# Two unused pads of 128 bytes among the SBUF tiles of a spatial mixing stage

## The chip, the core and the metric

The kernel runs on one core of one Trainium2 chip, as one launch. The metric is device time in microseconds, and what is compared is the median of several runs. Five engines work side by side and meet at semaphores: TensorE (PE in the profile; its weight loads are listed apart as PEld), VectorE (DVE), ScalarE (ACT), GpSimd (POOL) and SyncE (SP). Here SP only issues DMAs; POOL and ACT issue some as well.

SBUF is the on-chip memory from which TensorE reads both operands of a matmul. A tile takes the same range of bytes in each of 128 partitions, so one start address per tile says where it lies. This document speaks of the start modulo 256 bytes, as "the place in the slot".

## The reference, cut to what matters

A two-dimensional Fourier transform (its real part), an expert layer with the ELU nonlinearity, and a gated layer whose gate mixes the 3072 positions of a sequence with one 3072 by 3072 matrix. There are 4 sequences of 256 numbers per position. The last function holds the stage that is changed, the einsum.

```python
X = np.fft.fft(np.fft.fft(x, axis=1), axis=2).real          # x: 4 x 3072 x 256
h = X.reshape(4 * 3072, 256) @ w_in                         # 256 -> 2048
x = np.where(h > 0, h, np.exp(np.minimum(h, 0)) - 1) @ w_out  # back to 256

def _moe2_ref(x, w_in, w_spatial, b_spatial, w_out):
    h = np.maximum(x @ w_in, 0.0)                           # 256 -> 1024
    u, v = (h[..., :512], h[..., 512:])
    v_n = (v - mean(v)) / np.sqrt(var(v) + 1e-06)
    v_s = np.einsum('ts,bsd->btd', w_spatial, v_n) + b_spatial[None, :, None]
    return (u * v_s) @ w_out                                # 512 -> 256
```

## The kernel before

The kernel is written in one order per engine by hand (a manual schedule): what stands earlier in the program is issued earlier on its engine, and semaphores carry the dependencies. It has three stages.

1. *First transforms* (to about 120 us). Folded rows of x are multiplied by tables of cosines and sines (`to`, `te`) with plain float32 matmuls, at lines 399 to 418, in tiles named pa.
2. *Expert layer and the first half of the gated layer* (to about 1196 us). Twelve blocks of 1024 positions go through eight steps each. Every product here is made by `matmul3` (line 207), three float32r matmuls on operands split into a high and a low part: high by high, low by high, high by low. Its outputs are named pe and po (function s1), acc (s2), pv (v_piece) and pu (u_piece). Four steps of this stage also hold two matmuls each in tiles named own, whose weights are a tile of 8 columns, self (line 847). The first block's second product uses plain float32 matmuls at line 713. The normalised v and the gate's other factor u go to DRAM.
3. *Spatial stage* (to the end). The 3072 by 3072 matrix is cut into 3 by 3 blocks, and for each of two pairs of sequences the 18 block products of the direct way are replaced by 15 products of sums of blocks (PRODUCTS). With 2 chunks of 512 output positions and 4 steps of 256 input positions that gives 2 x 15 x 2 x 4 = 240 units. A unit has 8 calls of `matmul3`, so 24 matmuls of 128 x 128 weights and 512 columns.

For a unit, SP loads one to three tiles raw (512 KB each), DVE adds them (line 1004), ScalarE casts the sum to whi (line 1014) and DVE subtracts to get wlo (line 1020). The tiles vhi and vlo come in the same way once for two units. In the matmuls whi and wlo are the moving operand (`rhs`) and vhi and vlo the weights (`lhsT`), written to PSUM tiles named a. When a sum is complete, DVE multiplies it by u, it is split into gh and gl (lines 1081, 1085), and `project` multiplies it by the weights wo2: there gh and gl are the moving operand.

The SBUF tiles of this stage come from pools that are opened, before the expert layer has ended, at the right-hand (upper) end of SBUF, and each new pool lies below the one before: gq (gh, gl), wq (whi, wlo), cp (wo2), th (vhi, vlo), raw, and vt for the last block of the stage before. Each of their tiles is a multiple of 2048 bytes, so all tiles in one pool have the same place in the slot. The sums, u and the bias come from other pools at the left-hand end.

Of the kernel before, what the change touches and what calls it, by code (L numbers as in the profile page):

```python
# [9 lines left out]
F32 = mybir.dt.float32  # L10
# [5 lines left out]
P = 128  # L16
# [12 lines left out]
HB = BLK // 2  # L29
# [115 lines left out]
def fourier_ffn_gated_kernel(ctx: ExitStack, tc: tile.TileContext, t, out: bass.AP):  # L145
# [138 lines left out]
    with ExitStack() as ph:  # L284
        pool = lambda n, **k: ph.enter_context(tc.tile_pool(name=n, reuse_waits="tile", **k))
# [283 lines left out]
    def pool(name, stack=ffn, **k):  # L569
        return stack.enter_context(tc.tile_pool(name=name, reuse_waits="tile", **k))  # L570
# [381 lines left out]
    def pool(name, **k):  # L952
        return ctx.enter_context(tc.tile_pool(name=name, reuse_waits="tile", **k))

    gq = pool("gq", bufs=1, side="right")
    wq = pool("wq", bufs=1, side="right")
    cp = pool("cp", bufs=1, side="right")
    th = pool("th", bufs=VB, side="right")
    rp = pool("raw", bufs=1, side="right")
# [393 lines left out]
```

## Time and profile before

| | |
|---|---|
| Median of 3 runs | 2643.21 us (2640.79 to 2643.89) |
| The profiled execution | 2641.98 us |
| Its span, first to last instruction | 2640.2 us |
| TensorE busy, share of the span | 2615.8 us, 99% |
| DVE busy | 2038.1 us, 77% |
| ScalarE busy | 1262.5 us, 48% |
| GpSimd busy | 495.1 us, 19% |
| Read from and written to HBM | 399.68 MB and 172.06 MB, 217 GB/s over the span |
| The chain that ended last | 91% of it on TensorE |

The busy time of an engine is the time in which it has at least one instruction under way. Matmuls are pipelined, so the mean duration of one (389 ns for 512 columns) is longer than the distance between the starts of two that follow each other. The distance is what a stream of matmuls costs. It is read from a list of instructions in order of time, or as the length of a window divided by the matmuls that start in it.

### The profile page before, as it was taken

The page shows a single profiled execution, that of the slowest core. Times are in us where ns is not written, and L with a number is a line of the kernel's source. Part 1 is how long each engine was busy: PE and PEld are TensorE (multiplying, and loading weights), DVE is VectorE, ACT ScalarE, POOL GpSimd, SP SyncE. Part 2 cuts the span into 40 slices and gives each one's busy share as a digit, 9 for nine tenths or more (in the row PEclk, how much of TensorE's full clock was granted, in tenths as well). Part 3 has the DMA queues.
Part 4 walks back from the last instruction along what each step waited for, and adds up shares of the span by engine and source line. Part 5 has one row for each costly group of instructions (what it writes and reads, how often), then busy time and mean ns, then how long its engine had stood idle before and what let it go on. Part 6 is the DMA issues. An engine that isn't in the chain of part 4 may idle for free.

```text
span 2640.2 us, 31514 instructions
## 1 busy us (share of the span) xinstructions
PE 2615.8 (99%) x11270; PEld 2110.0 (80%) x11270; DVE 2038.1 (77%) x2311; ACT 1262.5 (48%) x1558; POOL 495.1 (19%) x908
## 2 busy tenths in 40 slices
PE   8999999999999999999999999999999999999999
PEld 4557888888888888888888888888888888888877
DVE  8899888888888888866677767678774776776686
ACT  3457777777777777763323333233223233222332
POOL 1101124544552344442010100010000000000000
PEclk9999999999999999999999999999999999999999
DMA  9702546777775666679697897879576867778683
GB/s 348 220 17 66 176 136 140 160 168 146 132 166 178 142 146 155 144 182 343 225 360 240 273 291 278 286 241 337 182 271 239 286 234 240 256 247 286 228 296 107
DMA packets 223618, 565.46 MB, mean 214 GB/s; under 512 B 33960, under 2 KB 46777, under 8 KB 222820
## 3 DMA queue, kind: packets, MB, share of 16 engines
q1 hardware_dynamic: 172846, 457.69, 49.3%
q0 software_dynamic: 49056, 103.89, 20.9%
q8 instruction: 88, 1.44, 0.2%
q10 hardware_dynamic: 1558, 1.87, 0.2%
q14 instruction: 70, 0.57, 0.1%
HBM read 399.68 MB, written 172.06 MB: 217 GB/s over the span
## 4 chain that ended last, share of the span: by engine, by line
PE 91%; ACT 1%; DVE 1%; issue 1%; DMA 1%; DVEq 0%; ACTq 0%; SPq 0%
PE a L213 18%; PE a L214 18%; PE a L212 18%; PE acc L214 6%; PE acc L213 6%; PE acc L212 6%; PE acc L713 2%; PE pe L212 2%; PE pe L214 2%; PE pe L213 2%; PE po L214 2%; PE po L212 2%; PE po L213 2%; PE pv L212 1%; PE pv L214 1%; PE pv L213 1%
## 5 line engine op out<-in xcount | busy, mean ns | idle before, releaser
L214 PE MATMUL a<-whi,vlo 128*128 128x512 f32 x1920 | 746.9, 389 | 0.0
L213 PE MATMUL a<-wlo,vhi 128*128 128x512 f32 x1920 | 746.9, 389 | 0.0
L212 PE MATMUL a<-whi,vhi 128*128 128x512 f32 x1920 | 746.9, 389 | 0.0
L1014 ACT CAST whi<-raw 128x1024 fp32r<-128x1024 f32 x240 | 252.6, 1053 | 803.3 <-PE a L214 394.3
L1020 DVE TENSOR_TENSOR wlo<-raw,whi 128x1024 fp32r<-128x1024 f32 x240 | 293.6, 1224 | 358.5 <-ACT whi L1014 358.4
L214 PEld LDWEIGHTS a<-whi,vlo 128*128 128x128 f32 x1920 | 360.4, 188 | 74.9
L213 PEld LDWEIGHTS a<-wlo,vhi 128*128 128x128 f32 x1920 | 360.4, 188 | 74.9
L212 PEld LDWEIGHTS a<-whi,vhi 128*128 128x128 f32 x1920 | 360.4, 188 | 74.8
L693 DVE TENSOR_TENSOR glo<-h,ghi 128x2048 fp32r<-128x2048 f32 x88 | 217.3, 2469 | 117.2 <-ACT ghi L689 117.2
L1004 DVE TENSOR_TENSOR raw<-raw 128x1024 f32<-128x1024 f32 x240 | 294.2, 1226 | 14.2 <-DMA raw<-in_wT 10.9
L212 PE MATMUL acc<-ghi,big 128*128 128x512 f32 x704 | 273.9, 389 | 0.0
L214 PE MATMUL acc<-ghi,big 128*128 128x512 f32 x704 | 273.9, 389 | 0.0
L213 PE MATMUL acc<-glo,big 128*128 128x512 f32 x704 | 273.9, 389 | 0.0
L1059 POOL DMA_DIRECT2D u<-u x24 | 20.3, 845 | 1108.8 <-DVE sum L1076 663.4
L672 ACT ACTIVATE e<-h 128x2048 f32<-128x2048 f32 x96 | 183.6, 1912 | 54.4 <-DVE h L666 24.0
L816 POOL DMA_DIRECT2D v<-v x216 | 195.3, 1297 | 42.4 <-DVE v L777 22.7
L682 DVE SCALAR_TENSOR_TENSOR h<-e,h 128x2048 f32<-128x2048 f32 x88 | 201.0, 2285 | 0.0
L676 ACT ACTIVATE e<-e 128x2048 f32<-128x2048 f32 x96 | 183.8, 1915 | 0.2
L689 ACT CAST ghi<-h 128x2048 fp32r<-128x2048 f32 x88 | 167.1, 1899 | 16.8 <-DVE h L682 16.8
L213 PEld LDWEIGHTS acc<-glo,big 128*128 128x128 f32 x704 | 132.2, 188 | 27.7
L212 PEld LDWEIGHTS acc<-ghi,big 128*128 128x128 f32 x704 | 132.1, 188 | 27.7
L214 PEld LDWEIGHTS acc<-ghi,big 128*128 128x128 f32 x704 | 132.1, 188 | 27.3
(184 smaller groups left out, 3937.4 us busy)
## 6 DMA issues: line engine op xcount, KB each, us to landing
raw<-in_wT SPq DMA_DIRECT2D x480, 512.0 KB, 5.5
vlo<-v SPq DMA_DIRECT2D x120, 512.0 KB, 5.3
v<-v SPq DMA_DIRECT2D x224, 256.0 KB, 2.7
v<-v POOLq DMA_DIRECT2D x216, 256.0 KB, 6.1
u<-uu SPq DMA_DIRECT2D x96, 256.0 KB, 2.0
u<-u POOLq DMA_DIRECT2D x24, 1024.0 KB, 10.0
out<-sum SPq DMA_DIRECT2D x46, 256.0 KB, 2.4
v<-vl POOLq DMA_DIRECT2D x40, 256.0 KB, 13.3
```

The costliest lines, as they stand in the source:

```text
L212: nc.tensor.matmul(acc, lhsT=w[0], rhs=x[0], start=start, stop=False, skip_group_check=more)
L213: nc.tensor.matmul(acc, lhsT=w[0], rhs=x[1], start=False, stop=False, skip_group_check=more)
L214: nc.tensor.matmul(acc, lhsT=w[1], rhs=x[0], start=False, stop=stop, skip_group_check=more)
L672: nc.scalar.activation(e, st[s]["h"], AF.Relu, scale=-1.0)
L676: nc.scalar.activation(e, e, AF.Exp, scale=-1.0)
L682: nc.vector.scalar_tensor_tensor(out=g, in0=e, scalar=-1.0, in1=h, op0=ALU.add, op1=ALU.max)
L689: nc.scalar.copy(st[s]["hi"], st[s]["h"])
L693: nc.vector.tensor_tensor(lo, st[s]["h"], st[s]["hi"].bitcast(F32), op=ALU.subtract)
L816: nc.gpsimd.dma_start(dst, v, accum_op=ALU.add)
L1004: nc.vector.tensor_tensor(res, total, y, op=ALU.add if sg > 0 else ALU.subtract)
L1014: nc.scalar.copy(hi, total)
L1020: nc.vector.tensor_tensor(lo, total, hi.bitcast(F32), op=ALU.subtract)
```

## The change

Two pools with one tile each are added. A tile has HB // 16 = 32 float32 numbers, 128 bytes, in each partition, and nothing ever reads or writes it. The pool top is opened above gq, the pool below_wq between wq and cp.

```diff
+    pool("top", bufs=1, side="right").tile([P, HB // 16], F32, name="top")
     gq = pool("gq", bufs=1, side="right")
     wq = pool("wq", bufs=1, side="right")
+    pool("below_wq", bufs=1, side="right").tile([P, HB // 16], F32, name="below_wq")
     cp = pool("cp", bufs=1, side="right")
     th = pool("th", bufs=VB, side="right")
     rp = pool("raw", bufs=1, side="right")
```

In the built program the instructions are the same ones in the same order on every engine, with the same waits. What differs is the start address of the tiles on the right-hand side in the spatial stage, and of vt:

| Tiles | Start modulo 256, before | after |
|---|---|---|
| gh, gl (moving in the projection) | 224 | 96 |
| whi, wlo (moving in the products) | 224 | 96 |
| wo2 (weights in the projection) | 224 | 224, 256 bytes lower |
| vhi, vlo (weights in the products) | 224 | 224, 256 bytes lower |
| raw, vt | 224 | 224, 256 bytes lower |
| sums, u, bias (left-hand end) | 128 | 128, not moved |

For comparison, places that the change leaves alone: in the expert layer the operands of pe, po, acc, pv and pu all start at 128, weights and moving ones alike. In own the weights self start at 32 and the moving operand at 128. In the first transforms the table to starts at 64, and the weights start at many places, in steps of 8 bytes. DVE's tile h lies by turns in three tiles, two at 128 and one at 160.

## Rows read from the trace of the kernel before

**Rows 1.** The page: TensorE's busy time, and its clock in 40 slices.

```profile
PE 2615.8 (99%) x11270; PEld 2110.0 (80%) x11270; DVE 2038.1 (77%) x2311; ACT 1262.5 (48%) x1558; POOL 495.1 (19%) x908
...
PEclk9999999999999999999999999999999999999999
```

**Rows 2.** Busy time by stretch; first numbers: stretch, its length, then each engine.

```profile
0.00:120.00 120.00, 109.03 (x330) 60.58 (x331) 108.90 (x193) 48.85 (x123) 20.09 (x31) 1.00 0.92 298
120.00:1196.00 1076.00, 1068.74 (x4579) 858.39 (x4578) 911.41 (x997) 769.01 (x921) 403.41 (x784) 1.00 0.60 143
1196.00:2636.00 1440.00, 1437.18 (x6361) 1190.37 (x6359) 1017.35 (x1121) 444.27 (x515) 71.61 (x94) 1.00 0.77 261
...
1300.00:2500.00 1200.00, 1200.00 (x5296) 993.64 (x5295) 847.66 (x929) 370.58 (x426) 57.59 (x67) 1.00 0.77 263
```

**Rows 3.** What TensorE waited for, whole span: us in total, times, longest.

```profile
PE pa L418 <- DMA to<-in_to: 8.3, 1, 8.3
PE a L213 <- DVE gl L1085: 2.8, 2, 2.1
PE pe L212 <- DVE q L661: 2.3, 4, 0.8
```

**Rows 4.** Order of time, spatial stage: start us, us; TensorE, then weight loads.

```profile
1299.52 0.39 PE L212 MATMUL a<-whi,vhi 128*128 128x512 f32 x1
...
1300.20 0.39 PE L212 MATMUL a<-whi,vhi 128*128 128x512 f32 x1
...
1300.88 0.39 PE L212 MATMUL a<-whi,vhi 128*128 128x512 f32 x1
...
1300.21 0.19 PEld L213 LDWEIGHTS a<-wlo,vhi 128*128 128x128 f32 x1
```

**Rows 5.** Order of time, the short matmuls at the end, first and last of ten.

```profile
2629.93 0.28 PE L212 MATMUL a<-gh,wo2h 128*128 128x256 f32 x1
...
2631.01 0.28 PE L212 MATMUL a<-gh,wo2h 128*128 128x256 f32 x1
```

**Rows 6.** TensorE by line and form: count, busy us, mean ns of one.

```profile
L214 PE MATMUL a<-whi,vlo 128*128 128x512 f32 x1920 | 746.9, 389 | 0.0
...
L213 PE MATMUL acc<-glo,big 128*128 128x512 f32 x704 | 273.9, 389 | 0.0
...
L212 PE MATMUL pu<-x2h,wi2h 128*128 128x512 f32 x192 | 74.7, 389 | 0.0
...
L214 PE MATMUL pv<-wi2h,x2l 128*128 128x512 f32 x192 | 74.7, 389 | 0.0
...
L213 PE MATMUL a<-gl,wo2h 128*128 128x512 f32 x184 | 71.7, 390 | 2.1 <-DVE gl L1085 2.1
...
L213 PE MATMUL a<-gl,wo2h 128*128 128x256 f32 x16 | 4.6, 290 | 0.7 <-DVE gl L1085 0.7
```

**Rows 7.** Order of time, expert layer, round one pair of own.

```profile
227.20 0.39 PE L212 MATMUL po<-xhi,woh 128*128 128x512 f32 x1
...
227.65 0.39 PE L214 MATMUL po<-xhi,wol 128*128 128x512 f32 x1
227.88 0.63 PE L847 MATMUL own<-big,self 128*8 128x512 f32 x2
228.34 0.39 PE L212 MATMUL acc<-ghi,big 128*128 128x512 f32 x1
```

**Rows 8.** Order of time, first transforms; like instructions in a row are merged.

```profile
60.67 5.32 PE L399 MATMUL pa<-to,q 128*128 128x384 f32 x16
65.83 2.75 PE L399 MATMUL pa<-te,q 128*128 128x386 f32 x8
68.42 5.32 PE L399 MATMUL pa<-to,q 128*128 128x384 f32 x16
73.58 2.75 PE L399 MATMUL pa<-te,q 128*128 128x386 f32 x8
```

**Rows 9.** Order of time, expert layer, a stretch with unequal steps.

```profile
427.84 0.40 PE L213 MATMUL pe<-xlo,big 128*128 128x512 f32 x1
...
428.30 0.40 PE L212 MATMUL po<-xhi,woh 128*128 128x512 f32 x1
428.54 0.39 PE L213 MATMUL po<-xlo,woh 128*128 128x512 f32 x1
428.76 0.39 PE L214 MATMUL po<-xhi,wol 128*128 128x512 f32 x1
...
430.15 0.39 PE L214 MATMUL acc<-ghi,big 128*128 128x512 f32 x1
```

**Rows 10.** DMA issues: count, KB each, median us from issue to landing.

```profile
raw<-in_wT SPq DMA_DIRECT2D x480, 512.0 KB, 5.5
vlo<-v SPq DMA_DIRECT2D x120, 512.0 KB, 5.3
```

**Rows 11.** DVE: wlo by line on the page; glo by tile, ns min/median/max.

```profile
L1020 DVE TENSOR_TENSOR wlo<-raw,whi 128x1024 fp32r<-128x1024 f32 x240 | 293.6, 1224 | 358.5 <-ACT whi L1014 358.4
...
L693 DVE TENSOR_TENSOR glo<-h,ghi x88: 2283/2293/5025, 214.0 to 1161.5; 128x2048 fp32r<-128x2048 f32 x88
```

## The prediction

> **What bounds the kernel now.** [...] The table by stage says where: the first transforms take 120 us, the expert layer 1076 us, the spatial stage 1440 us, and in the last of these TensorE is busy for 1437.2 us [rows 2]. The list of what TensorE waits for names nothing inside the spatial stage but one pair of waits of 2.8 us for DVE's gl, and no wait at all between 1300 and 2500 us [rows 3]. So the stage lasts as long as its matmuls take to stream. The other engines have room: DVE is busy for 1017 of the 1440 us and ScalarE for 444 [rows 2].
>
> What one matmul costs there is not its listed mean of 389 ns, which holds the latency of a pipelined instruction, but the distance from one start to the next. Between 1300 and 2500 us, 5296 matmuls start: 1200 / 5296 = 226.6 ns each [rows 2]; seven starts in a row say the same, 1299.52 to 1300.88 is 1.36 us for six [rows 4]. The short matmuls of 256 columns at the end start 0.12 us apart (2629.93 to 2631.01 is 1.08 us for nine) [rows 5]. [...]
>
> **The change part by part.** *Instructions.* The pads are reserved and never used, so nothing is added, removed or moved, and every instruction waits for the same semaphores as before. Cost: nothing, with no cover needed.
>
> *The matmuls.* The stage has 3 x 1920 matmuls of the products, 3 x 184 of the projection and 3 x 16 short ones, 6360 [rows 6]. All of them change alike: whi, wlo, gh and gl go to start 96 in a slot of 256 bytes, and the weights vhi, vlo and wo2 stay at 224. So 1 ns more or less per matmul is 6.4 us on the path that sets the end. How many ns? The trace of before has moving operand and weights at the same place in the slot in every full-width float32r matmul: 224 and 224 in the spatial stage, 128 and 128 in the expert layer. Two things can be read from that.
>
> First, the place itself does nothing: in the expert layer, at 128 and 128, acc, pu and pv have the same 389 ns mean as the products at 224 and 224 [rows 6], and settled they start as far apart (227.20 to 227.65 is 0.45 us for two) [rows 7].
>
> Second, the distance between the two operands is tried only in corners. The eight matmuls own have weights of 8 columns that start at 32, against big at 128. Around one pair, the matmul before, during which the first of these weights is loaded, is followed after 0.23 us (227.65 to 227.88), and the two own matmuls take 0.46 us together (227.88 to 228.34) [rows 7]. Neither is a shorter step. [...] The plain float32 matmuls of the first stage have weights scattered over the slot in steps of 8 bytes against tables at 64: sixteen of them start over 5.16 us (60.67 to 65.83), 322.5 ns each, and the next runs give the same 5.16 us [rows 8]. [...] But these stream at half the rate of float32r, so they excuse the address and do not acquit it.
>
> The bounds follow. [...] Upwards: the nearest row of a disturbed stream stands at 427.84 to 430.15 us, where ten matmuls start 2.31 us apart in all, 231 ns each, with single steps between 0.22 and 0.24 [rows 9]; 4.4 ns x 6360 = 28 us. I take zero, since the own pair and the scattered float32 weights are the only rows in which the distance changes, and neither lowers a step, nor raises one beyond what a disturbed stream shows anyway.
>
> *Loads and casts.* The tiles raw, vlo and vhi move by 256 bytes, so they keep their place in the slot; sizes, queues and order of the 480 loads of raw (5.5 us to land) and 120 of vlo are unchanged [rows 10]. Zero. DVE and ScalarE now write whi, wlo, gh and gl at 96 while they read at 224. DVE has a row for such a mix: glo<-h,ghi reads h from three tiles in turn, two at 128 and one at 160, and its median of 2293 ns is 10 ns off its minimum [rows 11]. Even a tenth more on wlo (240 x 1224 ns = 294 us) would be 29 us on an engine with 423 us free in the stage [rows 2, 11]. Zero on the path.
>
> The sum: 2640.2 us span + 0 = 2640.2, and with the 1.8 us that the profiled execution has outside its span, 2642.0. The median of the three runs is 1.2 us above, 2643.2, so I predict 2643.
>
> **The rivals.** *A, the distance frees the stream.* The next weights begin to load within 0.01 us of each matmul's start (1300.20 and 1300.21) [rows 4], so both reads set out together, and today from the same place in the slot. [...] In part, with the shortest step of rows 9 (0.22 us, about 224 ns, 2.7 ns less): 2643 - 17 = 2626.
> [...]
>
> *B, the distance breaks the stream's step.* Today the steps settle at 226.6 ns and stay there; after a disturbance they run at 231 ns for some ten matmuls before they settle [rows 9]. If the settled state needs operands at equal places, each spatial matmul stays at 231: 2643 + 28 = 2671. For it: every full-width pair in the trace lies equally, so no row shows that it can settle otherwise, and own's two steps average 0.23 rather than under it. Against it: plain float32 settles with any distance. It decides from 0.8 ns per matmul, which is 5 us.
> [...]
>
> *C, the tiles' new places change who waits.* The tiles shift by up to 256 bytes over those of the stage before. The waits are the same in the built program, so this is ruled out, and so is that the pads miss their mark: the starts are 96 and 224.
>
> **How the numbers follow.** A measurement of this kernel can tell 0.2%, 5.3 us, from no change. No effect on the path: 0.64, inside 2638 to 2648. A: 0.16, half of it beyond 2626. B: 0.20, a quarter of it beyond 2671. So faster 0.16, same 0.64, slower 0.20. The range reaches from A's part size to B's price, 2626 to 2671, and leaves out 0.08 + 0.05.
>
> **What would show it.** Right: some 5296 matmuls again between 1300 and 2500 us, and DVE's wlo near 1224 ns. [...] B would show as fewer, 5195 at 231 ns, with TensorE still waiting for nothing. If the step is unchanged and the time is not, my step about loads and casts is wrong, and the list of waits would name the engine.

## The result: slower, by 1.4%

The changed kernel takes 2677.55 us (median of 4 runs, 2677.43 to 2683.21) against 2642.78 us for the kernel before (here also the median of 4 runs). The two medians are 1.3% apart; the ratio on record is 1.014, with a 95% interval from 1.0128 to 1.0152. I had forecast no change, with a range that ended at 2671. The profiled execution of the changed kernel was the longest of the four, 2683.21 us with a span of 2681.4 us; the other three lie within 0.3 us of 2677.5. Why one kernel has two times is taken up with the experiments. One execution of the experiments, with the pad of 64 bytes, ran for 5112 us at a mean granted clock of 0.883, where all others have 0.998 to 1.0, and is left out of what follows.

The page of the changed kernel, TensorE's totals and its clock in 40 slices, which answer to [rows 1]:

```profile
PE 2658.9 (99%) x11270; PEld 2110.6 (79%) x11270; DVE 2038.5 (76%) x2311; ACT 1261.3 (47%) x1558; POOL 494.0 (18%) x908
...
PEclk9999999999999999999999999999999999999999
```

TensorE is busy 43.1 us longer with the same 11270 matmuls at the same clock, and no other engine's busy time moved by more than 1.2 us. Busy time by stretch (stretch, length, then busy us and count of each engine) says where, beside [rows 2]:

```profile
120.00:1196.00 1076.00, 1068.95 (x4579) 858.47 (x4579) 911.52 (x998) 768.68 (x921) 402.90 (x784) 1.00 0.61 143
1196.00:2677.00 1481.00, 1478.89 (x6359) 1190.12 (x6357) 1016.99 (x1120) 443.40 (x515) 71.13 (x94) 1.00 0.75 254
...
1300.00:2500.00 1200.00, 1200.00 (x5145) 965.24 (x5144) 828.14 (x903) 357.45 (x408) 55.36 (x64) 1.00 0.76 257
```

The expert layer is as it was. Between 1300 and 2500 us, 5145 matmuls start instead of 5296: 1200 / 5145 = 233.2 ns a step, 6.6 ns more than before. The 6312 matmuls of full width make 6312 x 6.6 = 42 us of that, and the two profiled executions differ by 2683.21 - 2641.98 = 41.2 us. So the loss is in the step.

What TensorE waited for over the whole span, beside [rows 3], shows that no wait was added (the largest three):

```profile
PE pa L418 <- DMA to<-in_to: 8.3, 1, 8.3
PE a L213 <- DVE gl L1087: 2.3, 2, 1.6
PE pe L212 <- DVE q L661: 2.2, 4, 0.8
```

By line and form (count, busy us, mean ns of one), beside [rows 6], each product and projection matmul of the spatial stage is listed 6 ns longer, and those of the expert layer are not:

```profile
L214 PE MATMUL a<-whi,vlo 128*128 128x512 f32 x1920 | 758.4, 395 | 0.0
...
L213 PE MATMUL acc<-glo,big 128*128 128x512 f32 x704 | 273.9, 389 | 0.0
...
L213 PE MATMUL a<-gl,wo2h 128*128 128x512 f32 x184 | 72.8, 396 | 1.6 <-DVE gl L1087 1.6
```

In order of time (start us, duration us), beside [rows 4], the steps are no longer alike but go up and down by turns, 0.23 and 0.24:

```profile
1299.94 0.40 PE L214 MATMUL a<-whi,vlo 128*128 128x512 f32 x1
1300.18 0.39 PE L212 MATMUL a<-whi,vhi 128*128 128x512 f32 x1
1300.41 0.40 PE L213 MATMUL a<-wlo,vhi 128*128 128x512 f32 x1
1300.65 0.39 PE L214 MATMUL a<-whi,vlo 128*128 128x512 f32 x1
1300.88 0.40 PE L212 MATMUL a<-whi,vhi 128*128 128x512 f32 x1
```

### The profile page after: what moved, and what is told of

The parts are those of the page before. It is cut to its first block, busy times and chain, and to the rows that moved or that the text cites. A ratio compares the mean times of both kernels' runs of the same rounds, so it can differ in the third digit from the quotient of the medians.

```text
span 2681.4 us, 31514 instructions
## 1 busy us (share of the span) xinstructions
PE 2658.9 (99%) x11270; PEld 2110.6 (79%) x11270; DVE 2038.5 (76%) x2311; ACT 1261.3 (47%) x1558; POOL 494.0 (18%) x908
## 4 chain that ended last, share of the span: by engine, by line
PE 91%; ACT 1%; DVE 1%; issue 1%; DMA 1%; POOL 0%; SPq 0%; DVEq 0%; ACTq 0%; POOLq 0%
PE a L213 18%; PE a L214 18%; PE a L212 18%; PE acc L213 6%; PE acc L214 6%; PE acc L212 6%; PE acc L713 2%; PE pe L212 2%; PE pe L213 1%; PE pe L214 1%; PE po L212 1%; PE po L213 1%; PE po L214 1%; PE pv L212 1%; PE pu L212 1%; PE pu L214 1%
## 5 line engine op out<-in xcount | busy, mean ns | idle before, releaser
L213 PE MATMUL a<-wlo,vhi 128*128 128x512 f32 x1920 | 758.4, 395 | 0.0
L214 PE MATMUL a<-whi,vlo 128*128 128x512 f32 x1920 | 758.4, 395 | 0.0
L212 PE MATMUL a<-whi,vhi 128*128 128x512 f32 x1920 | 758.4, 395 | 0.0
L1022 DVE TENSOR_TENSOR wlo<-raw,whi 128x1024 fp32r<-128x1024 f32 x240 | 293.6, 1224 | 397.4 <-ACT whi L1016 397.3
```

The lines of the kernel that those rows point to most:

```text
L212: nc.tensor.matmul(acc, lhsT=w[0], rhs=x[0], start=start, stop=False, skip_group_check=more)
L213: nc.tensor.matmul(acc, lhsT=w[0], rhs=x[1], start=False, stop=False, skip_group_check=more)
L214: nc.tensor.matmul(acc, lhsT=w[1], rhs=x[0], start=False, stop=stop, skip_group_check=more)
L1022: nc.vector.tensor_tensor(lo, total, hi.bitcast(F32), op=ALU.subtract)
```

## The experiments

My theory now was rival B: what counts is the distance in the slot between a matmul's moving operand and the weights. Its rivals: the moving operand's own place (96) is bad, or the shift of the tiles as such is at work. In the tables a step is 1200 us divided by the matmuls that start between 1300 and 2500 us.

**Each pad alone.** The first run keeps the one line, the second the other.

```diff
+    pool("top", bufs=1, side="right").tile([P, HB // 16], F32, name="top")
     gq = pool("gq", bufs=1, side="right")
     wq = pool("wq", bufs=1, side="right")
```


> The pad top alone: gh, gl, whi, wlo and the weights vhi, vlo, wo2 all lie at 96 of 256, so the moving operands are where the change puts them, and the distance to the weights is 0 again. Theory D (the distance between the moving operand and the weights that are loaded meanwhile sets the step): the step is back at 226.6 ns, 5296 matmuls between 1300 and 2500 us, and the time is 2643 us. Theory P (the place of the moving operand, 96 instead of 224, sets it): 233.3 ns as in the changed kernel, 2677 to 2683 us.

```diff
     wq = pool("wq", bufs=1, side="right")
+    pool("below_wq", bufs=1, side="right").tile([P, HB // 16], F32, name="below_wq")
```


> The pad below_wq alone: moving operands stay at 224, weights go to 96, the distance is 128 again but with the moving operands where the kernel before has them. Theory D: 233.3 ns a step, 2677 to 2683 us. Theory P: 226.6 ns, 2643 us.

Busy time by stretch, first of the pad top alone and then of below_wq alone:

```profile
1300.00:2500.00 1200.00, 1200.00 (x5296) 993.96 (x5295) 847.72 (x929) 370.69 (x426) 57.59 (x67) 1.00 0.77 263
```
```profile
1300.00:2500.00 1200.00, 1200.00 (x5166) 972.95 (x5165) 829.68 (x905) 357.44 (x408) 56.09 (x65) 1.00 0.77 258
```

With moving operands and weights both at 96 the count is back at 5296 and the time at 2642.42 us (ratio 1.000, 0.9989 to 1.0011). With the moving operands where they always were and the weights at 96 it is 5166 matmuls, 232.3 ns, and 2679.4 us (1.014, 1.0111 to 1.0170). The place of the moving operand is out; the distance stands.

**Other distances.** The pad below wq alone, with another size: n is the bytes.

```diff
+    pool("below_wq", bufs=1, side="right").tile([P, n // 4], F32, name="below_wq")
     cp = pool("cp", bufs=1, side="right")
```


> A pad of 64 bytes below wq, no other: moving operands at 224, weights at 160, so the weights lie 64 bytes lower in the slot. Theory D, in the form that only equal places settle at 226.6 ns: between 229 and 238 ns a step, 2660 to 2700 us. Theory D, in the form that the slot has two halves of 128 bytes and only the half counts: 224 and 160 are in the same half, 226.6 ns, 2643 us. Theory P: 2643 us.

> A pad of 192 bytes below wq, no other: moving operands at 224, weights at 32. Theory D, only equal places settle at 226.6 ns: between 229 and 238 ns a step, 2660 to 2700 us, not necessarily the same as with a pad of 64, since which of two reads is ahead is turned round. Theory D with two halves of 128 bytes: 224 and 32 are in different halves, 233.3 ns, 2677 to 2683 us. Theory P: 2643 us.

> A pad of 32 bytes below wq alone: weights at 192, moving operands at 224, distance 32. If the step grows with the distance from equal places (226.7 ns at 0, 228.9 at 64, 232.4 to 233.3 at 128): between 226.7 and 229 ns, 2643 to 2656 us. If any unequal place unsettles the stream: 229 ns or more, 2656 to 2684 us. [...]

> A pad of 224 bytes below wq alone: weights at 0 of the next slot, moving operands at 224, which is the distance of 32 to the other side. If the step follows the distance modulo 256 smoothly (233.3 ns at 192): between 226.7 and 233.3 ns, 2643 to 2684 us. If only the size of the distance counts, the same as with the pad of 32 bytes.

> A pad of 256 bytes below wq alone: weights at 224 again, one whole slot lower. If the distance counts modulo 256 (or a part of it): 226.7 ns, 2643 us. If it counts modulo 512 or more, as it could if the slot were larger than 256 bytes: 229 to 238 ns, 2656 to 2700 us. If a shift of the tiles as such is at work, also not 2643 us.

> A pad of 96 bytes below wq alone: weights at 128, distance 96. Theory (any distance that is not 0 modulo 256 costs): 228 to 234 ns a step, 2653 to 2690 us. A distance that frees the stream would show as less than 226.7 ns and less than 2640 us.

> A pad of 160 bytes below wq alone: weights at 64, distance 160. Theory (any distance that is not 0 modulo 256 costs): 228 to 234 ns a step, 2653 to 2690 us. A distance that frees the stream: less than 226.7 ns, less than 2640 us.

A smaller distance than a pad between pools gives comes from using larger tiles from 16 bytes past their start:

```diff
+    def inner(x):
+        return x[:, 4 : 4 + 2 * TC].rearrange("p (z t) -> p z t", z=2)
...
-            hi = wq.tile([P, 2, TC], F32R, tag="whi", bufs=3, name="whi")
+            hi = inner(wq.tile([P, 2 * TC + 64], F32R, tag="whi", bufs=3, name="whi"))
```
(and the same for wlo)

> The tiles whi and wlo are 256 bytes larger each and used from 16 bytes past their start: moving operands of the products at 240, weights at 224, a distance of 16, less than any pad between pools gives. If every unequal place costs: 229 ns or more, 2656 us or more. If places within 32 bytes count as equal: 226.7 ns, 2643 us. If the step falls for a small distance: under 226 ns, under 2638 us.

| Distance, moving minus weights, bytes | Matmuls in 1200 us | Step, ns | Median, us | Ratio, 95% interval |
|---|---|---|---|---|
| 0 (before) | 5296 | 226.6 | 2642.78 | |
| 16 (products only) | 5188 | 231.3 | 2669.06 | 1.0102, 1.0073 to 1.0132 |
| 32 | 5144 | 233.3 | 2684.37 | 1.0157, 1.0128 to 1.0187 |
| 64 | 5244 | 228.8 | 2653.92 | 1.0096, 1.0053 to 1.0138 |
| 96 | 5144 | 233.3 | 2683.21 | 1.0156, 1.0126 to 1.0185 |
| 128 (below_wq alone) | 5166 | 232.3 | 2679.4 | 1.014, 1.0111 to 1.0170 |
| 160 | 5123 | 234.2 | 2689.05 | 1.0178, 1.0148 to 1.0208 |
| 192 | 5145 | 233.2 | 2682.8 | 1.0153, 1.0124 to 1.0183 |
| 224 | 5144 | 233.3 | 2682.84 | 1.0151, 1.0122 to 1.0181 |
| 256 | 5296 | 226.6 | 2642.68 | 1.0002, 0.9991 to 1.0013 |

Distances of 16, 32, 64 and 128 cost 2.2 to 6.7 ns a step and 256 costs nothing (226.6 ns), so within what was tried the distance counts modulo 256 bytes. The form with two halves of 128 bytes does not survive, since 64 costs and 32 costs as much as 128; nor does the cost grow smoothly with the distance. The side counts too: 64 and 192 bytes are equally far from equal places, and their traces have 228.8 and 233.2 ns. No distance that was tried gave a step under 226.6 ns, so none frees the stream, and rival A is out. At 64 there are two sorts of executions: four lie at 2653.6 to 2653.9 us, under the 2660 us that I had expected at the least, and three at 2679.6 to 2681.6. The median and the step in the row are of the first sort; the ratio is over both.

**Which weights: those loaded meanwhile, or the matmul's own?** Of the three matmuls of a `matmul3` (it begins at line 209, not 207 as stated above), (whi, vhi), (wlo, vhi) and (whi, vlo), either vlo alone or wlo alone is moved by 128 bytes.

```diff
     th = pool("th", bufs=VB, side="right")
+    pool("below_th", bufs=1, side="right").tile([P, HB // 16], F32, name="below_th")
+    tl = pool("tl", bufs=VB, side="right")
...
-                raw = th.tile([P, 2, HV], F32R, tag="vlo", name="vlo")
+                raw = tl.tile([P, 2, HV], F32R, tag="vlo", name="vlo")
```


> Only vlo (and raw, which TensorE does not read) is moved by 128 bytes, to 96; vhi, wlo and whi stay at 224. vlo is the weights of the third matmul of each three (line 214) and is loaded while the second (line 213) streams. If the clash is between a stream and the weights that are loaded meanwhile: the step that begins at line 213 is the long one, the two others 226 to 227 ns, and the mean is between 227 and 229 ns: 2645 to 2658 us. If it is a matter of the matmul's own weights: the step that begins at line 214 is the long one. If one disturbed step unsettles all three: 231 ns or more in each, 2671 us or more.

```diff
     wq = pool("wq", bufs=1, side="right")
+    pool("below_wq", bufs=1, side="right").tile([P, HB // 16], F32, name="below_wq")
+    wlp = pool("wl", bufs=1, side="right")
+    pool("below_wl", bufs=1, side="right").tile([P, HB // 16], F32, name="below_wl")
...
-        lo = x if key[0] == "v" else wq.tile([P, 2, TC], F32R, tag="wlo", bufs=3, name="wlo")
+        lo = x if key[0] == "v" else wlp.tile([P, 2, TC], F32R, tag="wlo", bufs=3, name="wlo")
```


> Only wlo is moved by 128 bytes, to 96; whi and all weights stay at 224. wlo is the moving operand of the second matmul of each three (line 213); the third (line 214) streams whi with vlo as its own weights while vhi is loaded, all at 224. With vlo alone moved, lines 213 and 214 were both long (232.0 and 233.5 ns) and line 212 was not (226.7). Theory 1 (a matmul is long when its moving operand lies unequally to its own weights or to those loaded meanwhile): line 213 long, 230 to 238 ns, lines 212 and 214 at 226 to 227; mean 228 to 230.5, 2650 to 2667 us. Theory 2 (a long step disturbs the next one too): lines 213 and 214 both long, mean 230 to 232, 2664 to 2677 us.

TensorE by line and form (count, busy us, mean ns), vlo alone and then wlo alone:

```profile
L214 PE MATMUL a<-whi,vlo 128*128 128x512 f32 x1920 | 762.2, 397 | 0.0
L213 PE MATMUL a<-wlo,vhi 128*128 128x512 f32 x1920 | 760.3, 396 | 0.0
L212 PE MATMUL a<-whi,vhi 128*128 128x512 f32 x1920 | 746.9, 389 | 0.0
```
```profile
L213 PE MATMUL a<-wlo,vhi 128*128 128x512 f32 x1920 | 758.4, 395 | 0.0
L212 PE MATMUL a<-whi,vhi 128*128 128x512 f32 x1920 | 750.5, 391 | 0.0
L214 PE MATMUL a<-whi,vlo 128*128 128x512 f32 x1920 | 746.8, 389 | 0.0
```

With vlo moved, line 213, which streams while vlo is loaded, is long by 7 ns, and line 214, whose own weights vlo is, while vhi at an equal place is loaded, by 8; line 212 is not. Taken from all starts in the trace, the steps that begin at lines 212, 213 and 214 are 226.7, 232.5 and 234.2 ns (the 232.0 and 233.5 of the second expectation are a little low). None of the three forms that I had written down says that. Either both relations count, or a long step makes the next one long. With wlo moved, line 213 is long, and line 214 right behind it has its old 389 ns, which speaks against the latter. Line 212 has 391, a mean over two stretches: in the first two steps in three are long and the third a little (235.8, 234.2 and 230.0 ns from lines 212, 213 and 214), in the second one in three (226.7, 234.2 and 225.8). The same instructions in order of time, at 1300 us and at 1600 us of that run:

```profile
1300.08 0.40 PE L213 MATMUL a<-wlo,vhi 128*128 128x512 f32 x1
1300.31 0.39 PE L214 MATMUL a<-whi,vlo 128*128 128x512 f32 x1
1300.54 0.40 PE L212 MATMUL a<-whi,vhi 128*128 128x512 f32 x1
1300.78 0.40 PE L213 MATMUL a<-wlo,vhi 128*128 128x512 f32 x1
...
1600.36 0.40 PE L213 MATMUL a<-wlo,vhi 128*128 128x512 f32 x1
1600.59 0.39 PE L214 MATMUL a<-whi,vlo 128*128 128x512 f32 x1
1600.82 0.39 PE L212 MATMUL a<-whi,vhi 128*128 128x512 f32 x1
1601.04 0.40 PE L213 MATMUL a<-wlo,vhi 128*128 128x512 f32 x1
```

Three steps take 0.70 us there and 0.68 us here. The times are 2665.72 us for vlo (1.0087, 1.0057 to 1.0116) and 2658.68 us for wlo (1.0067, 1.0045 to 1.0090). Busy time by stretch shows the two as well, 233.1 and 228.6 ns a step:

```profile
1200.00:1490.00 290.00, 290.00 (x1244) 233.42 (x1243) 207.98 (x225) 84.84 (x94) 23.31 (x25) 1.00 0.83 282
1510.00:2500.00 990.00, 990.00 (x4330) 811.60 (x4329) 685.58 (x742) 302.46 (x343) 36.75 (x46) 1.00 0.76 260
```

The change falls between them, at the first projection: its 24 matmuls have moving operand and weights at equal places and soon run at 226.7 ns a step, and the products behind them run in the second row from the start. At the start of the first stretch the products come out of an unsettled stream: the trace of the kernel before, where the order is the same, has steps of 228 to 251 ns between 1194.2 and 1198.2 us. So the places alone do not set the step, and what the stream ran in before most likely decides its row, here by 4.5 ns. "Both relations count" fits vlo alone and the second stretch of wlo alone; it does not fit the first stretch, where line 212, at equal places in both relations, is the longest. Which matmul pays is open.

**Another stage, and plain float32.** The spatial stage is left as before; in the expert layer 128 of the unused bytes of a tile are cut.

```diff
-    wmid = wp.tile([P, 4 * NF1], F32, name="wmid")[:, :NF1]
+    wmid = wp.tile([P, 2 * NF1], F32, name="wmid")[:, :NF1]
```


> The spatial stage as before; in the expert layer the tile wmid, 256 bytes of which 64 are used, is made 128 bytes, which moves wo, xhi, xlo and the tiles of e, h, ghi and glo from 128 to 0 of 256, while big stays at 128. So acc (weights big, 2112 float32r matmuls) and pe (weights big, 576) get a distance of 128, po (weights wo, moving xhi and xlo) stays at equal places, and the plain float32 matmuls of line 713 (weights big, moving e) get a distance of 128 too. If the distance sets the step of float32r everywhere: acc and pe 229 to 238 ns instead of 226.7, po near 227, the spatial stage 226.7, and 2688 x 6.7 ns = 18 us more, 2650 to 2668 us. If plain float32 is indifferent to it: line 713 stays at 429 ns. If the effect belongs to the spatial stage alone: 2643 us.

By line and form, acc, one line each of po and pe, then busy time by stretch, the spatial stage:

```profile
L212 PE MATMUL acc<-ghi,big 128*128 128x512 f32 x704 | 278.2, 395 | 0.0
L213 PE MATMUL acc<-glo,big 128*128 128x512 f32 x704 | 278.1, 395 | 0.0
...
L212 PE MATMUL po<-xhi,woh 128*128 128x512 f32 x192 | 76.3, 397 | 1.5 <-ACT woh L614 1.5
...
L213 PE MATMUL pe<-xlo,big 128*128 128x512 f32 x192 | 75.0, 391 | 0.0
...
1300.00:2500.00 1200.00, 1200.00 (x5296) 993.65 (x5295) 846.98 (x924) 371.61 (x425) 56.84 (x66) 1.00 0.78 265
```

acc has gone from 389 to 395 ns, the spatial stage has its 5296 matmuls, and the time is 2662.41 us (1.0083, 1.0053 to 1.0112), 22 us more than the 2640.83 us of the kernel before on the same chip. So the cost follows the operands into another stage. My expectation that po would stay near its old step failed: its first matmul rose from 390 to 397 ns although its places are equal, between long neighbours. The other way round, pe's second matmul has unequal places in both relations and rose by 1 ns only, from 390 to 391. So here too the distance slows the stretch, and not each matmul for itself. The plain float32 matmuls of line 713 are in order of time, first in this run, then in the kernel before:

```profile
216.34 3.59 PE L713 MATMUL acc<-e,big 128*128 128x512 f32 x8
219.37 0.79 PE L212 MATMUL pe<-xhi,big 128*128 128x512 f32 x1
```
```profile
210.97 3.59 PE L713 MATMUL acc<-e,big 128*128 128x512 f32 x8
214.00 0.79 PE L212 MATMUL pe<-xhi,big 128*128 128x512 f32 x1
```

Eight of them and the way to the next take 3.03 us in both, at a distance of 128 and of 0. So plain float32 shows no cost of this distance.

**Two times of one kernel.** Two kernels once more, unchanged.

> The kernel with a pad of 64 bytes below wq again, unchanged, for a second profiled execution: its executions came at 2653.7 or at 2680 us. If the stream of one kernel has several settled cycles, and which one it falls into is a matter of its start: a trace at 2680 us shows another repeating row of steps, mean 233 ns, throughout the stage, with the same instructions and no new waits. If the two times came from something else (a wait, a load): the steps are 228.9 ns as in the first trace.

> The changed kernel again, unchanged: one execution was at 2683.2 us with steps of 229 and 238 ns in turn (mean 233.3), three at 2677.5 us, of which there is no trace. If there are several settled cycles: a trace at 2677.5 us shows another row of steps with a mean near 232.4 ns, as the pad below_wq alone had at 2677.2 us. If it is a wait: the same 233.3 ns and a wait that is shorter by 6 us.

The changed kernel came at 2675.28 and 2676.08 us this time (1.0133, 1.0103 to 1.0162), and the trace, of the first, has another row of steps:

```profile
1300.00:2500.00 1200.00, 1200.00 (x5165) 972.87 (x5164) 828.79 (x904) 358.39 (x410) 56.09 (x65) 1.00 0.76 258
```

5165 matmuls are 232.3 ns each, where the first trace had 5145 and 233.2 ns. 0.9 ns x 6312 is 5.7 us, and the two profiled executions differ by 7.9 us, so most of the difference between these two is the step as well. The kernel before came at 2640.83 us in this round, 2 us less than in the first, which is about what is left. The pad of 64 bytes came at 2653.5 to 2655.5 us three times (1.0050, 1.0028 to 1.0073), with 5245 matmuls, so of its executions near 2680 us there is no trace, and what they do is open.

## Why the prediction was wrong

*That the stage lasts as long as its matmuls stream* was right, and it is why 6.6 ns showed in full: TensorE still waits for nothing between 1300 and 2500 us.

*That instructions, waits, loads and casts cost nothing* was right. wlo, written at 96 from operands at 96 and 224, still takes 1224 ns on DVE.

*The step that failed is the choice of zero for the matmuls.* In its place the runs show 5.7 to 6.6 ns a matmul, 36 to 42 us over the 6312 of full width. I wrote that the own pair and the plain float32 weights, the only rows in which the distance changes, "neither lowers a step, nor raises one beyond what a disturbed stream shows anyway". Two things were wrong in it.

First, I read the own pair for what rival A needed, a shorter step, and not for what it showed. Its two matmuls take 0.46 us, and before them a settled stream has 0.45 us for two [rows 7]; at hundredths of a microsecond that cannot be told apart. But the trace of before has one more line for the eight matmuls of own, by line and form, which I did not set beside the 389 ns of [rows 6]:

```profile
L847 PE MATMUL own<-big,self 128*8 128x512 f32 x8 | 2.5, 397 | 0.0
```

They are listed 8 ns longer, and by the starts in the trace the two of [rows 7] are stepped at 234 and 235 ns, in a stream that had run at 226 and 227 and waited for nothing. The seven steps behind them are 228 to 236 ns before it settles again. The matmul before, during which own's weights are loaded, was short (226 ns), and own's two, whose own weights lie at a distance of 96 from big, were long. Put down as a disturbance, this was most likely the effect itself: line 214 with vlo alone was long in the same way (234.2 ns), with its own weights at an unequal place.

Second, I let plain float32 speak for float32r, while noting that it streams at half the rate (322.5 ns for 384 columns [rows 8], against 226.6 ns for 512). The run on the expert layer shows it indifferent, with 3.03 us for eight at distances of 128 and 0, where float32r at a distance of 128 is listed 6 ns longer (acc, 395 ns against 389), so it was no evidence.

*Rival B had the condition and the place,* with 0.20 where it should have led: the trace held no float32r pair at unequal places but own, so nothing in it showed that the settled step survives. Its picture of a stream that stays unsettled was only half right: the stream does settle, but into rows of steps with a higher mean (232.3 or 233.2 ns in the changed kernel, against 226.6). Its price was 4.4 ns from the unsettled stretch of [rows 9], 28 us, 2671. Measured are 5.7 to 6.6 ns, 2675 to 2683. The range ended at that price instead of beyond it; the own pair, about 235 ns each, would have put it at 8.4 x 6360 = 53 us, 2696.

*Rival A* fell to the sweep: no distance that was tried gives a step under 226.6 ns. No run shows the gain of 17 us that I gave for its part size, nor any beyond it.

## What to carry to other kernels

When float32r matmuls set the time, give the moving operand and the weights the same start modulo 256 bytes; equal places cost 226.6 ns for 512 columns here, and every other distance that was tried 1 to 3.4% more. A pad or a tile of odd size anywhere above in the pool shifts all that lies below it, so look at the addresses after such an edit even where the order and the waits are unchanged. A listing in hundredths of a microsecond hides a few ns; the mean by line and form, or a count over a long window, does not. And when a row is called on as evidence against one rival, read it once more for the other.

## What the runs showed of the hardware

- A float32r matmul of 512 columns starts 226.6 ns after the one before when operand and weights start equally modulo 256 bytes, and 228.8 to 234.2 ns after it, on average, at the eight distances of 16 to 224 that were tried. The distance of 64 was the cheapest in its two traces (228.8), but three of its executions took as long as those of other distances (2680 us).
- Moving vlo alone or wlo alone by 128 bytes is enough to slow the stream (2665.72 and 2658.68 us). Which relation of a matmul counts, to its own weights or to those loaded meanwhile, is open: vlo alone lengthens one matmul of each sort, and neither relation explains the first stretch of wlo alone.
- In the changed kernel the stream ran in a repeating row of unequal steps (229 or 230 and 237 or 238 ns by turns, 233.2 on average), and in a second trace of it in another (232.3 ns on average). With wlo alone a row of 233.1 ns gave way to one of 228.6 in mid-stage, behind 24 matmuls at equal places.
- Plain float32 shows no cost of the distance: eight matmuls and the way to the next take 3.03 us at 128 and at 0. For float32r the places of the two operands matter to each other, by 6.6 ns a matmul between the changed kernel and the one before (233.2 and 226.6 ns); how the two reads meet was not shown by any run.
- What in the chip makes 256 bytes the period was not shown by any run.
